# Converting double-precision weights piece by piece: three ScalarE and three VectorE instructions, or two, two and one GpSimd add

## The chip, the core and the metric

The kernel runs on one core of a Trainium2 chip. Five engines work side by side and meet only at semaphores: TensorE (PE in the profile; its weight loads are the row PEld), VectorE (DVE), ScalarE (ACT), GpSimd (POOL) and SyncE (SP), which here only issues DMAs. Each engine takes its instructions strictly in the order in which they stand in its own queue, so an instruction that waits holds everything behind it. The metric is the device time of one execution in microseconds: before the change the median of three runs is 786.03 us (785.67 to 788.26).

## The reference

Two blocks follow each other. The first is a linear-attention recurrence with a 40x40 state for each of 4 batches and 8 heads, over 768 steps. The second is a feed-forward block on the 3072 rows that come out of it, with the hardswish activation.

```python
for t in range(S):                                   # attention, state (B, H, D, D)
    y[:, :, t] = np.einsum('bhd,bhde->bhe', rt, state)
    Sa = np.einsum('bhde,bhe->bhd', state, at)
    state_decay = state * wt[:, :, None, :] - np.einsum('bhd,bhe->bhde', Sa, bt)
    state = state_decay + np.einsum('bhd,bhe->bhde', vt, kt)
...
h = x @ w_in                                         # x (3072, 320), w_in (320, 2048)
g = h * np.clip(h + 3.0, 0.0, 6.0) / 6.0
return (g @ w_out).astype(np.float32)                # w_out (2048, 320)
```

The inputs of the attention are float32. The two weight matrices are float64, since they are scaled by a float64 factor and not cast. The engines work in float32, so the kernel has to turn 2 x 655,360 doubles into float32 on the chip, and this conversion is what the change is about. A double is two 32-bit words: the low word holds 32 bits of the mantissa, the high word the sign, 11 bits of exponent and the top 20 bits of the mantissa.

## The kernel before, in words

**Attention.** The sequence is cut into chunks of 64 steps. A unit is one chunk of two batches; there are 24 units, in groups of `NU` = 4. For each unit `prepare` makes the products that do not need the state (running products of the decay `w` by two scans, lines 571 and 582; scaled `a`, `b`, `k`; score matrices, masked by the predicated copy of line 546), and `step` then carries the state along. For each group of four units a triangular system is inverted on VectorE (`invert`): 30 rounds of a product into `prod` (line 769) and a sum into `x` (line 775), each waiting for the one before, then two 32x32 block transposes (lines 778 and 783) into `tb` and `tt`. `third_block` finishes the inverse into `tinv` with small matmuls.

**Feed-forward.** `expand` multiplies a unit's transposed rows `xt` with `win` and `win2` (line 1124), lines 1139 and 1140 apply the activation into `gt`, and `contract` multiplies with `wout` (line 1165). These matmuls are dealt out between the attention's as soon as a unit and the weights are there.

**Weights.** `weight_pieces` cuts both matrices into `PIECES` = 20 pieces of 128 partitions x 512 doubles; 0 to 4 and 10 to 14 belong to `w_in`, the others to `w_out`. A piece is loaded raw into whatever buffer is free for a while (`raw_homes`: the tiles of `raw`, `tinv`, `F`, `x`, `fb`, `tt`, and parts of `win` and `wout` that are not yet filled), and its float32 values go to their place in `win`, `win2` or `wout`, called `to`. In the raw buffer low and high words alternate, so each is read with a step of 8 bytes. A raw buffer may be loaded again only when the piece in it is finished; the list `free` in `raw_homes` says which piece each later load has to wait for (piece 8 for piece 2, 9 for 3, 10 for 4, 11 for 5, 15 for 8, 16 for 9, 19 for 13). The loads are issued by SP.

Per piece the kernel before runs six instructions of 128 x 512. On ScalarE, `power` makes the power of two of each element in `to`: line 386 scales the top 16 bits down to the exponent field, lines 387 and 388 use Prelu with a huge and a tiny slope to saturate and shift it. On VectorE, line 371 replaces sign-and-exponent bits of the high word by a constant (`tensor_scalar`, two bit operations), line 374 adds the low word times 2^-32 (`scalar_tensor_tensor`), which leaves the mantissa as a float32, and line 362 multiplies it with the power in `to`.

**Order.** Everything is written out by hand; no scheduler moves it. `load_weights` is a generator that yields after `power`, after the last instruction of the piece before, and after each of the two other VectorE instructions. So on VectorE the last instruction of piece n comes right before the first two of piece n+1. The generator is advanced from lists of places: `STEPS` and `POWERS` beside the first inversion, `PLAN` after it, and `by_twos`. The first two pieces and the beginning of the third stand among the 30 rounds of the first inversion. The counters `converted` and `powered` decide at build time when a matmul or a load may stand in a queue.

**Other things on the way.** `seconds` gives a second pair of input tiles `W` and `A` (tile `WA`, in the buffer with the tag `x`, which piece 12 uses before) and has GpSimd fill their padding (line 191). GpSimd also copies scan results (lines 599, 600, 602), keeps the carried decay (lines 869 and 870, which line 871 on VectorE waits for before it scales the state), copies `tb` into `tinv` (lines 818 and 819), clears `U` (line 899), multiplies `KBt` (line 690) and `yg` (line 1054 in the first group, 1029 later).

Of the kernel before, what the change touches and what calls it, by code (L numbers as in the profile page):

```python
# [8 lines left out]
F32 = mybir.dt.float32  # L9
I32 = mybir.dt.int32  # L10
U32 = mybir.dt.uint32
I16 = mybir.dt.int16
ALU = mybir.AluOpType
AF = mybir.ActivationFunctionType
# [3 lines left out]
P = 128  # L18
# [1 line left out]
HB = BL // 2  # L20
L = 32
SLOT = 64
EXP = 916


def _ap(ap, extra, dims):
# [5 lines left out]
def kernel(  # L32
# [42 lines left out]
    nc = tc.nc  # L75
# [12 lines left out]
    const = ctx.enter_context(tc.tile_pool(name="const", bufs=1))  # L88
# [52 lines left out]
    def ps_pair(*dims):  # L141
# [21 lines left out]
        out=ident[:], in_=ones, pattern=[[1, P]],  # L163
# [15 lines left out]
    nc.vector.memset(three[:], 3.0)  # L179
    warm = const.tile([P, 1], F32, name="warm")  # L180
    nc.scalar.activation(out=warm[:], in_=three[:], func=AF.Relu)
    low = const.tile([P, 3], F32, name="low")
    for i, x in enumerate((EXP - 1792.0, -1792.0 * 2 ** 23, -15.0 / 32.0)):
        nc.vector.memset(low[:, i:i + 1], x)


    AHEAD = NU + 1
# [11 lines left out]
    def seconds():  # L199
        t = inv.tile([P, 2, H, SLOT], F32, name="WA1", tag="x", bufs=1)  # L200
        for i, name in enumerate("WA"):
            others[name] = padded(t[:, i], name)
# [58 lines left out]
    for i, (x, y) in enumerate([(0, DFF // 2), (0, NJ // 2)]):  # L261
        for n, z in enumerate((x, y)):
# [4 lines left out]
            name = ("WA", "BK")[i][n]  # L267
# [46 lines left out]
    def load_weights():  # L314

        todo, homes = weight_pieces(), raw_homes()  # L320
        done, issued = [], [0]
        upcoming = []

        def load():
            if issued[0] == min(PIECES, limit[0]):
                return False
            if not upcoming:
                upcoming.append(next(homes))
            raw, before = upcoming[0]
            if before is not None and before not in done:  # L330
                return False
            upcoming.clear()
            issued[0] += 1
            out, loads = next(todo)
            for to, src in loads(raw):
                nc.sync.dma_start(out=to, in_=src)
            loaded.append((out, raw))
            return True

        while load():  # L340
            pass
        refill.append(load)
        phase[0] = 0
        yield
        before = None
        for n in range(PIECES + 1):
            now = None
            if n < PIECES:
                while load():
                    pass  # L350
                out, raw = now = loaded[n]
                hi = raw[:, :, :, 1]
                if powered[0] == n:
                    power()
                    phase[0] = 1
                    yield
            if before:
                to, raw_m = before
                m = raw_m[:, :, :, 1].bitcast(F32)
                if len(to.shape) == 4:  # L360
                    m = m.rearrange("p n (j c) -> p n j c", c=to.shape[3])
                nc.vector.tensor_tensor(out=to, in0=m, in1=to, op=ALU.mult)
                converted[0] += 1
                done.append(n - 1)
                while load():
                    pass
                phase[0] = 2
                yield
            before = now
            if now:  # L370
                nc.vector.tensor_scalar(hi, hi, 0xFFFFF, 0x100000, ALU.bitwise_and, ALU.bitwise_or)
                phase[0] = 3
                yield
                nc.vector.scalar_tensor_tensor(hi.bitcast(F32), raw[:, :, :, 0], 2.0 ** -32, hi, ALU.mult, ALU.add)
                phase[0] = 4
                yield

    def power():

        to, raw = loaded[powered[0]]  # L380
        powered[0] += 1
        top = raw.rearrange("p n c t -> p n (c t)").bitcast(I16)[:, :, 3::4]
        if len(to.shape) == 4:
            top = top.rearrange("p n (j c) -> p n j c", c=to.shape[3])
        bits = to.bitcast(I32)
        nc.scalar.activation(out=bits, in_=top, func=AF.Identity, bias=low[:, 2:3], scale=1.0 / 16.0)
        nc.scalar.activation(out=to, in_=bits, func=AF.Prelu, bias=low[:, 0:1], scale=-1.0, alpha=2.0 ** -40)
        nc.scalar.activation(out=bits, in_=to, func=AF.Prelu, bias=low[:, 1:2], scale=-2.0 ** 63,
                             alpha=2.0 ** -40)

    def weight_pieces():

# [51 lines left out]
    def fetch(name, i, engine=None):  # L444

        if i is None or i >= NK:
            return
        x, crossed = {"W": (w, 0), "A": (a, 0), "B": (b, 0), "K": (k, 0), "R": (r, 1),
                      "V": (v, 1)}[name]
        if name == "V":  # L450
            t = values[i % AHEAD]
        else:
            t = placed.get((name, i))
            if (name, i) == ("R", 1):
                t = others["K"]
            if (name, i) == ("W", NU + 1):
                t = values[NU]
            t = t if t is not None else (others if i < 2 * NU and i % 2 and name != "R" else inputs)[name]
        g, p = names[i]
        engines = engine or nc.sync  # L460
        for q in range(2):
            engine = engines[q] if isinstance(engines, tuple) else engines
            y = x[2 * p + q, :, g * BL:(g + 1) * BL, :]
            rows = slice(q * BL, (q + 1) * BL)
            if crossed:
                for s in range(2):
                    engine.dma_start(out=t[rows, 4 * s:4 * s + 4, 0:D],
                                     in_=y[s::2].rearrange("h t e -> t h e"))
            else:
                engine.dma_start(out=t[rows, :, 0:D], in_=y.rearrange("h t e -> t h e"))  # L470
        data[i][name + "N"] = t
# [890 lines left out]
    for t, line in enumerate(plan):  # L1362
        if t == 8:
            begun_ffn()
            ring.clear()
            ring.extend([("one", 1), ("whole", 2)])
        for name, *amounts in line:
            run(chains[name[0]], 0, 0, *map(int, amounts))
        limit[0] = {3: 15, 8: 17, 9: PIECES}.get(t, limit[0])
        if t == BEGIN - 2:  # L1370
            seconds()
            third.clear()
            second_group = by_twos(NU, 3, 0, 1.25)
        if t == BEGIN:
            fetch("A", NU + 1)
            fetch("W", NU + 3)
        if t == BEGIN + 2:
            fetch("V", NU)
            fetch("V", NU + 1)
            fetch("R", NU)  # L1380
        if t == BEGIN + 1:

            for name in "BK":
                others[name] = second(name)
                fetch(name, NU + 1)
        if t >= BEGIN - 2:
            pieces(3 if t < BEGIN else 1.5 if t < BEGIN + 3 else 0)
        if t >= BEGIN:
            next(second_group)
# [158 lines left out]
```

## Time and profile before

| what | value |
|---|---|
| median of the runs | 786.03 us (785.67 to 788.26, 3 runs) |
| the profiled execution's own time | 785.4 us |
| its span (first to last instruction) | 783.7 us |
| busy in the span: PE, DVE, ACT, POOL | 725.0, 486.6, 320.2, 171.9 us |
| line 362, DVE, 20 instructions | 14.34 us, first at 47.5, last at 131.1 us |
| line 371, DVE, 20 instructions | 408 to 1511 ns, medians 417 to 426 |
| line 374, DVE, 20 instructions | 668 to 978 ns, medians 680 to 698 |
| lines 386, 387, 388, ACT, 20 each | medians about 762, 722, 722 ns |
| lines 1029 and 1054, POOL, 128 x 512 product of two tiles | 1272 ns (20), 1278 and 1606 ns (2) |

Times in views are microseconds from the start of the span; an arrow names who released a wait. A group line gives the line of the program, the engine, the operation, the tiles (written <- read), the shape, the count, the busy time, the mean of one, and the idle time of the engine just before with what ended it. In the row of forty slices each slice is 19.6 us long.

### The profile page before, as it was taken

To read this page: it belongs to the slowest core of one execution; us is meant where nothing else is said; L and a number is where in the kernel's file an instruction comes from. 1 tells how busy PE (TensorE), PEld (TensorE's weight loads), DVE (VectorE), ACT (ScalarE), POOL (GpSimd) and SP (SyncE) were. 2 spreads that over 40 slices of the span, in tenths; PEclk is the share of its full clock that TensorE was granted. 3 is DMA by queue.
4 is the path that set the end of the run, shared out by engine and by line. 5 is a ranking of instruction groups with operands and counts; after the bars stand their busy time and mean duration, and the time that the engine had idled before them with its cause. 6 is when DMAs were issued, how large, how long until landed. Compare 5 with 4: busy or idle time off the path is not lost.

```text
span 783.7 us, 32780 instructions
## 1 busy us (share of the span) xinstructions
PE 725.0 (93%) x14552; PEld 613.3 (78%) x14552; DVE 486.6 (62%) x951; ACT 320.2 (41%) x664; POOL 171.9 (22%) x321
## 2 busy tenths in 40 slices
PE   5636788999999989999999999999999999999998
PEld 3625677878878778888788888888888888888886
DVE  7899967688546699345888336887436972223110
ACT  2386865324445334443334543334543234412211
POOL 6403111222232304121304212203212111110000
PEclk9855899999999999999999999999999999999999
DMA  9684554311333312223213223213221101110000
GB/s 123 116 202 123 113 168 69 68 27 35 58 59 63 67 33 48 50 49 66 41 38 58 46 51 64 44 30 60 49 55 39 26 5 30 30 29 10 12 20 18
DMA packets 174205, 44.87 MB, mean 57 GB/s; under 512 B 157424, under 2 KB 172784, under 8 KB 174064
## 3 DMA queue, kind: packets, MB, share of 16 engines
q1 hardware_dynamic: 169760, 42.03, 27.5%
q8 instruction: 115, 1.88, 1.0%
q10 hardware_dynamic: 4304, 0.74, 0.6%
q14 instruction: 26, 0.21, 0.1%
HBM read 34.08 MB, written 3.93 MB: 49 GB/s over the span
## 4 chain that ended last, share of the span: by engine, by line
PE 77%; DVE 10%; issue 6%; DMA 2%; ACT 2%; POOL 2%; SPq 1%; POOLq 0%; ACTq 0%; DVEq 0%
PE h L1124 27%; PE o L1165 25%; PE pair L1021 4%; PE pair L524 4%; PE pair L496 2%; PE one L486 2%; DVE prods L571 2%; PE pair L884 2%; PE pair L925 1%; PE pair L717 1%; DVE prod L769 1%; PE pair L964 1%; DVE x L775 1%; PE pair L980 1%; PE one L906 1%
## 5 line engine op out<-in xcount | busy, mean ns | idle before, releaser
L1124 PE MATMUL h<-xt,win 128*128 128x128 f32 (+1 forms) x2304 | 248.7, 281 | 4.5 <-DVE gt L1140 4.5
L1124 PEld LDWEIGHTS h<-xt,win 128*128 128x128 f32 (+1 forms) x2304 | 229.3, 191 | 22.6 <-issue 4.2
L1165 PE MATMUL o<-wout,gt 128*128 128x320 f32 x768 | 230.5, 443 | 0.0
L1165 PEld LDWEIGHTS o<-wout,gt 128*128 128x128 f32 x768 | 138.4, 190 | 50.9 <-issue 0.2
L1140 DVE SCALAR_TENSOR_TENSOR gt<-gt,h 128x512 f32<-128x512 f32 x96 | 62.0, 680 | 73.4 <-ACT gt L1139 73.4
L1139 ACT ACTIVATE gt<-h,three 128x512 f32<-128x512 f32 x96 | 62.9, 687 | 102.8 <-PE h L1124 102.3
L546 DVE COPY_PREDICATED area<-mask,pair 128x512 f32<-128x512 int32 x56 | 40.4, 724 | 62.2 <-PE pair L524 52.8
L769 DVE TENSOR_TENSOR prod<-x 128x30 f32<-128x30 f32 (+9 forms) x180 | 65.5, 364 | 8.9 <-POOL x L754 3.3
L775 DVE TENSOR_TENSOR x<-x,prod 128x30 f32<-128x30 f32 (+9 forms) x180 | 64.3, 357 | 5.5
L1029 POOL TENSOR_TENSOR yg<-ys,gam 128x512 f32<-128x512 f32 x20 | 25.4, 1272 | 126.1 <-DVE ys L1028 83.2
L690 POOL TENSOR_TENSOR KBt<-K,rgt 128x320 f32<-128x320 f32 x22 | 19.1, 870 | 151.4 <-ACT rgt L679 139.9
L571 DVE TENSOR_TENSOR_SCAN prods<-area,start 128x528 f32<-128x528 f32 x24 | 40.8, 1703 | 9.7 <-ACT area L567 9.6
L1028 DVE TENSOR_TENSOR ys<-pair,ys 128x512 f32<-128x512 f32 x20 | 13.8, 690 | 49.8 <-PE pair L1021 40.8
L862 ACT ACTIVATE RT<-pair 128x512 f32<-128x512 f32 x22 | 13.1, 597 | 54.5 <-PE pair L496 54.4
L722 ACT ACTIVATE EV<-pair 64x320 f32<-64x320 f32 x44 | 18.9, 430 | 36.9 <-PE pair L717 36.5
L1021 PE MATMUL pair<-area,KBt 64*64 64x104 f32 x1280 | 33.1, 252 | 0.0
L1183 ACT ACTIVATE ob<-o 128x320 f32<-128x320 f32 x22 | 9.6, 437 | 56.2 <-PE o L1165 37.8
L837 ACT ACTIVATE tinv<-pair 32x256 f32<-32x256 f32 x48 | 18.0, 375 | 34.7 <-PE pair L827 34.2
L582 DVE TENSOR_TENSOR_SCAN area<-area,start 128x528 f32<-128x528 f32 x24 | 31.1, 1297 | 0.8
L1021 PEld LDWEIGHTS pair<-area,KBt 64*64 64x64 f32 x1280 | 29.1, 133 | 1.4
L950 POOL COPY area<-V 128x320 f32<-128x320 f32 x20 | 9.1, 455 | 84.6 <-DVE area L612 52.9
L600 POOL COPY rgam<-prods 128x256 f32<-128x256 f32 x22 | 24.9, 1131 | 0.0
(286 smaller groups left out, 1049.9 us busy)
## 6 DMA issues: line engine op xcount, KB each, us to landing
V<-in_v_dram SPq DMA_DIRECT2D x96, 40.0 KB
out_dram<-ob SPq DMA_DIRECT2D x47, 80.0 KB
R<-in_r_dram SPq DMA_DIRECT2D x92, 40.0 KB
B<-in_b_dram SPq DMA_DIRECT2D x42, 80.0 KB
K<-in_k_dram SPq DMA_DIRECT2D x42, 80.0 KB
W<-in_w_dram SPq DMA_DIRECT2D x37, 80.0 KB
A<-in_a_dram SPq DMA_DIRECT2D x37, 80.0 KB
xt<-yg SPq DMA_DIRECT2D x72, 40.0 KB
```

Source lines behind the costliest of these rows:

```text
L524: nc.tensor.matmul(out=o[i][half(q), n ^ (2 * q * placed), :], lhsT=lhs[half(i, D), n ^ (2 * q * swap), half(q)], rhs=rhs[half(i, D), n, h ...
L546: nc.vector.copy_predicated(out=x[:].rearrange("p (i h) t -> p i h t", i=2), mask=mask8, data=o[2])
L571: nc.vector.tensor_tensor_scan(out=prods[:].rearrange("p r m i -> p (r m i)"), data0=wm[:, 0:SCAN], data1=start[:], initial=0.0, op0=ALU.m ...
L582: nc.vector.tensor_tensor_scan(out=back, data0=back, data1=start[:], initial=0.0, op0=ALU.mult, op1=ALU.add)
L769: nc.vector.tensor_tensor(out=pv, in0=_ap(x[:], (i + 1) * L + i, [[L, n], [0, i]]), in1=_ap(x[:], i * L, [[0, n], [1, i]]), op=ALU.mult,)
L775: nc.vector.tensor_tensor(out=rest, in0=rest, in1=pv, op=ALU.add)
L1021: nc.tensor.matmul(out=both[q][half(s), pr, :], lhsT=o[name][half(q), h * D:h * D + SLOT], rhs=beside[name][half(q), 4 * rs + 2 * (s ^ (q ...
L1029: nc.gpsimd.tensor_tensor(out=yg[:], in0=m["ys"][:].rearrange("p r q t -> p r (q t)"), in1=o["G"][:], op=ALU.mult)
L1124: nc.tensor.matmul(out=hp[c][:, i, :], lhsT=lhsT, rhs=rhs, start=(begun[c] == 0), stop=(begun[c] == 3 * NQ - 1))
L1139: nc.scalar.activation(out=gt[:], in_=hp[c][:], func=AF.Relu, bias=three[:], scale=1.0)
L1140: nc.vector.scalar_tensor_tensor(out=gt[:], in0=gt[:], scalar=6.0, in1=hp[c][:], op0=ALU.min, op1=ALU.mult)
L1165: nc.tensor.matmul(out=op[:], lhsT=gts[c][:, n, :], rhs=wout[:, c * HJ + r * NQ + n, :], start=((split or r == 0) and c == 0 and n == 0), ...
```

## The change

The conversion is written in another way, with five instructions per piece.

- On ScalarE, `power` has two copies instead of three activations: the low word times 2^-29 in place (uint32 read, int32 written, so the 3 lowest mantissa bits of the float32 that is to come), and the high word, read as if it were a float32, times 2^-112 into `to`. The second lowers the exponent field so that it fits.
- On VectorE, the first instruction is a `scalar_tensor_tensor`: high word AND sign bit, OR the scaled low word, into the high word. The second is a `tensor_scalar`: `to` shifted left by 3 bits. The third (line 362) is gone.
- On GpSimd, an integer add of the two, `tensor_tensor`, 128 x 512 int32, into `to`, stands where line 362 stood in the program. It is the instruction that finishes the piece.
- The constants in the tile `low` and their three memsets are gone.
- `seconds()` is called two lines of the plan later, at `BEGIN` instead of `BEGIN - 2`.

```diff
-EXP = 916
...
-    low = const.tile([P, 3], F32, name="low")
-    for i, x in enumerate((EXP - 1792.0, -1792.0 * 2 ** 23, -15.0 / 32.0)):
-        nc.vector.memset(low[:, i:i + 1], x)
...
             if before:
                 to, raw_m = before
-                m = raw_m[:, :, :, 1].bitcast(F32)
+                m = raw_m[:, :, :, 1].bitcast(I32)
                 if len(to.shape) == 4:
                     m = m.rearrange("p n (j c) -> p n j c", c=to.shape[3])
-                nc.vector.tensor_tensor(out=to, in0=m, in1=to, op=ALU.mult)
+                nc.gpsimd.tensor_tensor(out=to.bitcast(I32), in0=m, in1=to.bitcast(I32), op=ALU.add)
                 converted[0] += 1
...
             if now:
-                nc.vector.tensor_scalar(hi, hi, 0xFFFFF, 0x100000, ALU.bitwise_and, ALU.bitwise_or)
+                nc.vector.scalar_tensor_tensor(hi, hi, 0x80000000, raw[:, :, :, 0], ALU.bitwise_and, ALU.bitwise_or)
                 phase[0] = 3
                 yield
-                nc.vector.scalar_tensor_tensor(hi.bitcast(F32), raw[:, :, :, 0], 2.0 ** -32, hi, ALU.mult, ALU.add)
+                bits = out.bitcast(U32)
+                nc.vector.tensor_scalar(bits, bits, 3, None, ALU.logical_shift_left)
                 phase[0] = 4
                 yield
...
         to, raw = loaded[powered[0]]
         powered[0] += 1
-        top = raw.rearrange("p n c t -> p n (c t)").bitcast(I16)[:, :, 3::4]
+        lo, hi = raw[:, :, :, 0], raw[:, :, :, 1].bitcast(F32)
         if len(to.shape) == 4:
-            top = top.rearrange("p n (j c) -> p n j c", c=to.shape[3])
-        bits = to.bitcast(I32)
-        nc.scalar.activation(out=bits, in_=top, func=AF.Identity, bias=low[:, 2:3], scale=1.0 / 16.0)
-        nc.scalar.activation(out=to, in_=bits, func=AF.Prelu, bias=low[:, 0:1], scale=-1.0, alpha=2.0 ** -40)
-        nc.scalar.activation(out=bits, in_=to, func=AF.Prelu, bias=low[:, 1:2], scale=-2.0 ** 63,
-                             alpha=2.0 ** -40)
+            hi = hi.rearrange("p n (j c) -> p n j c", c=to.shape[3])
+        nc.scalar.activation(out=lo.bitcast(I32), in_=lo, func=AF.Copy, scale=2.0 ** -29)
+        nc.scalar.activation(out=to, in_=hi, func=AF.Copy, scale=2.0 ** -112)
...
         if t == BEGIN - 2:
-            seconds()
             third.clear()
             second_group = by_twos(NU, 3, 0, 1.25)
         if t == BEGIN:
+            seconds()
             fetch("A", NU + 1)
             fetch("W", NU + 3)
```

## The prediction

> **What bounds the kernel now.** I read the forty slices first, then busy time by stretch, then the chain of waits and the instructions in order of time inside the stretches in which weights are converted (41 to 131 us).
>
> ```profile
> PE   5636788999999989999999999999999999999998
> DVE  7899967688546699345888336887436972223110
> ACT  2386865324445334443334543334543234412211
> POOL 6403111222232304121304212203212111110000
> ```
>
> From about 134 us on TensorE is full. The busy time by stretch shows it in microseconds (columns PE, PEld, DVE, ACT, POOL, granted clock, DMA):
>
> ```profile
> 41.00:61.10 20.10, 5.04 (x80) 4.46 (x80) 18.91 (x52) 16.25 (x25) 0.00 (x0) 0.58 0.85 190
> 61.10:94.40 33.30, 23.76 (x856) 20.85 (x856) 31.43 (x52) 26.16 (x48) 10.81 (x21) 0.70 0.54 128
> 94.40:107.40 13.00, 10.20 (x216) 9.59 (x216) 8.91 (x17) 8.66 (x14) 0.71 (x3) 0.87 0.37 114
> 107.40:134.10 26.70, 24.57 (x480) 21.74 (x480) 21.34 (x36) 14.97 (x25) 3.46 (x5) 0.94 0.49 109
> 134.10:783.70 649.60, 637.12 (x12328) 536.12 (x12328) 371.98 (x729) 240.29 (x522) 134.98 (x231) 1.00 0.22 42
> ```
>
> In the last 650 us TensorE is busy for 637.1, and its queue has the same order in the changed kernel, so a shift of TensorE at 134 us is a shift of the end, one for one. All that can be won or lost lies before. There VectorE is the bound: 18.9 of 20.1 us beside the first inversion, 31.4 of 33.3 us after it. What TensorE waits for says where:
>
> ```profile
> PE lent L804 <- DVE tb L778: 10.1, 1, 10.1
> PE h L1124 <- DVE gt L1140: 2.7, 1, 2.7
> PE lent L1042 <- DVE state L1005: 1.9, 1, 1.9
> ```
>
> The first is the end of the inversion at 61.1 us; the second comes at 107.4 us, behind ScalarE's `gt` and, before it in that queue, six conversion instructions.
>
> **What a GpSimd product does to VectorE.** GpSimd is free (0.00 us busy in 41 to 61.1), so the add has room there. But look at the one product of the same size that runs among conversions, and at VectorE beside it:
>
> ```profile
> 111.43 1.61 POOL L1054 TENSOR_TENSOR yg<-ys,gam 128x512 f32<-128x512 f32 x1 [9.58 <-DMA raw_fb<-in_moe_w_out_dram]
> ...
> 111.21 0.68 DVE L362 TENSOR_TENSOR win<-raw_tt,win 128x512 f32<-128x512 f32 x1
> 111.81 1.51 DVE L371 TENSOR_SCALAR raw<-raw 128x512 uint32<-128x512 uint32 x1
> 113.36 0.69 DVE L374 SCALAR_TENSOR_TENSOR raw<-raw 128x512 f32<-128x512 uint32 x1
> ```
>
> The GpSimd product begins while line 362 runs and takes 1.61 us instead of its usual 1.27; line 371, usually 0.42 us, takes 1.51 and ends when the product has ended. So the two take turns: VectorE lost 1.09 us. The products of line 690 (0.86 us each) do the same to the inversion at 33.9 to 37.3 us, where instructions of 0.27 to 0.29 us take 0.75 to 0.87. Not all of VectorE is hit: line 703, which reads PSUM, keeps its 0.68 us beside line 690 at 32.0, and line 546 its 0.72 at 161.4.
>
> By the Trainium skill, "SBUF — State Buffer", section "SBUF: two separate sides", GpSimd and a VectorE instruction with two SBUF inputs, or in a mode that uses both ports, exclude each other for the whole instruction, and this is the rule that speaks against the change. The rows above agree; with 1.27 instead of 1.09 us for each, the sum below would be about 0.9 us higher.
>
> **The change, part by part.** Unit costs: line 362 takes 0.69 us, but behind a product of the inversion it costs 0.49 us (47.21 to 48.14, against the 0.44 from one round's instruction to the next), elsewhere 0.59 to 0.73 from start to start. Bit operations with two inputs in place of line 371 I take at line 374's 0.60 from start to start, the shift in place of line 374 at line 371's 0.33; within a piece they cancel. The integer add is not in the trace. Nearest is the product of two tiles, 1.27 us (line 1029), which I take, since it also reads two and writes one; the bounds are 0.73 (the one-input copy of line 950, 0.456 us for 320 columns, scaled to 512) and 2.5 (twice the product, as the add also reads with a step of 8 bytes, integers, in place).
>
> 41 to 61.1 us, every instruction on VectorE's chain: adds 0 and 1 each stop the inversion, 2 x 1.09 = +2.2; two line 362 go, -1.0; the third piece's first bit operation stands here and becomes the dearer one, +0.3. Sum **+1.5**.
>
> 61.1 to 79.1: no change. TensorE, at a clock of 0.50, is busy without a gap from 66.2 to 79.6 us and VectorE waits for it at 72.8 and 79.1 (0.72 us); five line 362 go and adds 2 to 6 come inside. If that cover were gone, the five adds less the five products would cost 5 x (1.09 - 0.65), 2.2 us.
>
> 79.1 to 94.4, VectorE without a gap up to the scaled state (line 871, 93.8), which TensorE's line 884 awaits: line 362 of pieces 7, 8 and 9 goes, -0.64 - 0.61 - 0.73; piece 10's first operation, +0.3. Add 7 is followed by two copies from PSUM (0.79 us), which leaves 0.35 of its 1.09; add 8 by lines 1050 and 888, also from PSUM (1.0 us), 0.2; add 9 by a bit operation, 1.09. GpSimd's queue is in order, so line 599's copies (85.1) now stand behind add 8, land on the scan of line 582 and cost about 0.5; line 869, which line 871 awaits, stands behind add 9, inside that add's price. Sum **+0.4**.
>
> 94.4 to 107.4: ScalarE's two pieces take 4.4 us from 101.1 to 105.5. A copy without a bias tile I take at 0.61 us (0.45 for line 878's 320 columns, plus 192 columns at the 0.81 ns by which lines 862 and 563 differ), so two pieces are 1.9 us shorter; but `gt` also needs the matmuls that end at 104.75, so it begins at 104.8 instead of 106.0. Sum **-1.2**.
>
> 107.4 to 134.1: the chain passes VectorE from `gt` (117.4) to the mask of line 546 (122.5): line 362 of piece 16, -0.6; piece 17's first operation, +0.3; add 16, partly behind line 1005 from PSUM, 0.7. Later adds stand beside a wait of 0.4 us. Sum **+0.4**.
>
> Costed at nothing: the three memsets (0.07 us each; VectorE then idles 1.38 us). `seconds()`: the padding of `WA` moves in GpSimd's queue from 100.2 us to behind add 15, about 116; the loads of `WA` do not touch the padding and wait for no GpSimd instruction, and TensorE reads the tile at 125.9. SP's queue keeps its order, but loads into used raw buffers now wait for an add; piece 8's starts at 66.7 us behind piece 2, whose add ends at about the same time as line 362 did, and ScalarE wants it at 82.4. Waits added to GpSimd: each add waits for VectorE and holds the copies, the clearing of `U` and `yg` behind it; of these only line 869 has someone waiting within a microsecond. Without GpSimd's slack each microsecond there would go to line 871.
>
> Total: 1.5 + 0.4 - 1.2 + 0.4 = **+1.1 us** on the profiled execution's 785.4 (span 783.7, 1.7 around it), 786.5. That execution lies 0.6 below the median of 786.03, so the forecast is 787.1 as a median.
>
> **The rivals.** (1) *The integer add is dearer than the float product.* Six adds lie on the path (0, 1, 7, 8, 9, 16), so each microsecond more costs six. From 1.5 us on, the sum passes 2.4 us and the kernel is measurably slower; at 2.0 us it is 787.1 + 6 x 0.73 = 791.5, at 2.5 us 794.5. For it: the form is in no row. Against it: every two-input GpSimd row has the same rate, 2.5 to 2.7 ns a column. The Trainium skill, "GPSIMD Engine Reference", section "Performance pitfalls for Q7 kernels", puts a dearer rate only beyond a step of 8 bytes, which this step does not exceed; no row here has such a step.
>
> (2) *The adds slip in for little, and the kernel is faster.* Without any turn-taking the stretches give -0.7, -1.7, -1.2 and -0.3, -3.9 us: 782.1. The losses I count are 5.0 us; if they come to less than 1.6, a third, it is measurably faster. For it: instructions that read PSUM are not stopped, and a waiting GpSimd may choose its gap. Against it: beside the inversion there is no such instruction for most of the time.
>
> (3) *SP falls behind.* From 106.5 to 154 us it issues nearly without a pause, and TensorE already waits 0.27 us for `B` at 149.8. If add 13 released the last raw buffer 2 us late (104.3 us before), 1.7 us would reach that wait: 788.8. A pause of 1.1 us at 116.3 stands against it.
>
> Beside these, the granted clock falls to half in steps of 3.4 us after pauses; one step more or less is 1.7 us either way.
>
> **How the numbers follow.** About 0.3%, 2.4 us, is what a measurement of this kernel can tell from none. My own sum, within that: 0.40. Rival 1: 0.28, rival 3 or a lost clock step: 0.10, together slower 0.38. Rival 2, with a won clock step: 0.22, faster. The likeliest is 787.1, its own range 784.5 to 788.4. The range of all, 781.8 to 793, leaves out about 0.06 below and 0.09 above (the add near its upper bound).
>
> **What would show it.** Right: line 362's successor on GpSimd at 1.2 to 1.7 us; rounds of the inversion of over 1 us beside the first two adds and line 778 starting at about 62.6; `gt` 1.2 us sooner after the rows have landed; line 1124 waiting 1.5 instead of 2.7 us. Wrong: line 778 before 61, adds above 1.7 us, or a new wait of TensorE for GpSimd or for a load.

## The result and the profile after

The changed kernel takes 790.59 us (median of 20 runs, 787.11 to 795.58), the kernel before in the same comparison 785.54 (20 runs, 783.90 to 788.26). The ratio is 1.0065, with a 95% interval of 1.0050 to 1.0081: about 5.1 us slower. That is inside the wide range on record (781.8 to 793), outside the narrower range of the forecast's own sum (784.5 to 788.4), and more than the 1.1 us forecast as likeliest. The profiled execution of the changed kernel took 790.17 us (span 788.2).

In the changed kernel GpSimd's add is line 358, VectorE's two bit operations are lines 367 and 371, ScalarE's two copies 382 and 383; from there on each line has a number smaller by 6 than before (871 is now 865). The forty slices, as before, of 19.7 us:

```profile
PE   5725789999999989999999999999999999999997
DVE  7899757688546699345898346887435982223110
ACT  2365543233454334453234543334533234412211
POOL 6416434322233303112304122304212201110000
```

The busy time by stretch (the window and its length, then PE, PEld, DVE, ACT and POOL with their counts of instructions, granted clock, DMA share and GB/s), cut where the same instructions stand that ended the stretches shown for the kernel before:

```profile
41.00:62.30 21.30, 5.34 (x80) 4.76 (x80) 20.03 (x50) 12.85 (x22) 2.63 (x2) 0.58 0.73 167
62.30:97.70 35.40, 23.71 (x856) 20.82 (x856) 29.73 (x45) 17.21 (x38) 20.72 (x30) 0.69 0.50 121
97.70:112.90 15.20, 12.10 (x216) 11.26 (x216) 7.43 (x12) 6.50 (x12) 5.68 (x5) 0.78 0.60 186
112.90:138.90 26.00, 23.38 (x480) 20.47 (x480) 20.15 (x30) 10.07 (x20) 11.56 (x13) 1.00 0.32 58
138.90:788.20 649.30, 635.51 (x12328) 535.10 (x12328) 371.74 (x728) 240.04 (x522) 134.80 (x231) 1.00 0.22 42
```

The stretches were 20.1, 33.3, 13.0, 26.7 and 649.6 us long and are now 21.3, 35.4, 15.2, 26.0 and 649.3. The last one keeps its length and its 12,328 matmuls: TensorE's shift at its start is the shift of the end, as the prediction read it. VectorE, which filled the second stretch before (31.4 of 33.3 us), now leaves 5.7 us of it free. It is no longer short of time there; it waits. What TensorE waits for between 60 and 170 us names the new link:

```profile
PE lent L798 <- DVE tb L772: 13.6, 1, 13.6
PE pair L518 <- ACT RT L856: 3.2, 1, 3.2
PE lent L1036 <- issue: 2.0, 1, 2.0
PE pair L711 <- DVE area L540: 1.7, 1, 1.7
PE pair L821 <- ACT zs L806: 1.6, 2, 1.1
PE h L1118 <- issue: 1.6, 1, 1.6
PE pair L1036 <- DVE area L540: 1.5, 1, 1.5
PE h L1118 <- DVE gt L1134: 1.4, 1, 1.4
PE pair L878 <- ACT UT L964: 1.3, 1, 1.3
```

The wait for ScalarE's `RT` was not there before. The instructions of all engines in order of time around it show where it comes from (an idle time stands in brackets, with who ended it):

```profile
92.44 0.69 DVE L367 SCALAR_TENSOR_TENSOR raw<-raw 128x512 uint32<-128x512 uint32 x1
93.05 0.42 DVE L371 TENSOR_SCALAR wout<-wout 128x512 uint32<-128x512 uint32 x1
93.50 0.65 ACT L382 ACTIVATE wout<-wout 128x512 int32<-128x512 uint32 x1 [4.96 <-DVE wout L371]
94.06 0.64 ACT L383 ACTIVATE win<-wout 128x512 f32<-128x512 f32 x1
94.60 0.58 ACT L905 ACTIVATE S<-one 128x512 f32<-128x512 f32 x1
94.78 1.29 POOL L358 TENSOR_TENSOR wout<-raw,wout 128x512 int32<-128x512 int32 x1 [3.70 <-ACT win L383]
95.08 0.59 ACT L856 ACTIVATE RT<-pair 128x512 f32<-128x512 f32 x1
...
95.72 0.69 PE L518 MATMUL pair<-RT,VT 40*64 40x64 f32 x32 [3.25 <-ACT RT L856]
...
96.10 0.69 DVE L367 SCALAR_TENSOR_TENSOR wout<-wout 128x512 uint32<-128x512 uint32 x1 [2.64 <-POOL wout L358]
...
96.71 0.48 DVE L865 TENSOR_TENSOR state<-state,scale 128x320 f32<-128x320 f32 x1
```

Read it from the top. VectorE's shift (line 371, 93.05) writes piece 9 into its place in `wout`. ScalarE has been idle for 4.96 us waiting for that shift, since its next instruction is the in-place copy (line 382) of piece 10. Behind the copy in ScalarE's queue stand `S` and `RT`; `RT` came at 90.19 us before and comes at 95.08, and TensorE waits 3.25 us for it. Meanwhile GpSimd's add of piece 9 (94.78) waits for ScalarE's line 383 of piece 10, and VectorE's next instruction (96.10) waits for that add, so the scaled state comes at 96.71 instead of 93.80 us. In the kernel before, `RT`, ScalarE's first instruction of piece 10 (line 386) and the scaled state stand without an idle time before them:

```profile
90.19 0.59 ACT L862 ACTIVATE RT<-pair 128x512 f32<-128x512 f32 x1
90.67 0.76 ACT L386 ACTIVATE win<-wout,low 128x512 int32<-128x512 int16 x1
...
93.80 0.48 DVE L871 TENSOR_TENSOR state<-state,scale 128x320 f32<-128x320 f32 x1
```

Pieces 9 and 10 have no element in common. Piece 10 lies raw in rows 4 to 7 of `wout`; the destination of piece 9 is columns 256 to 319 of rows 0 to 3 and of rows 8 to 11. Seen as one stretch from first to last element, it brackets the raw piece. That the program's waits go by this stretch is inferred from who waits for whom; the experiments below test it. Before the change only ScalarE and the last VectorE instruction wrote the destination, and both stood in an order in which no engine had to wait for another. Now VectorE's shift writes it ahead of ScalarE's work on piece 10, and the instruction that finishes it is on a third engine.

After the stall TensorE's granted clock is at one half for longer: 0.50 from 98 to 104 us, where the kernel before has 0.50 from 96 to 98 and 0.95 from 98 to 100. The 24 matmuls of `h` on line 1118 take 5.11 us from 99.64; before, the same 24 took 3.84 from 96.12. `gt` starts at 111.46 instead of 105.98 us, the mask at 126.68 instead of 121.77, and the end is 4.5 us later.

### The profile page after: what moved, and what is told of

It is laid out like the page before. It is cut to its first block, busy times and chain, and to the rows that moved or that the text cites. A ratio compares the mean times of both kernels' runs of the same rounds, so it can differ in the third digit from the quotient of the medians.

```text
span 788.2 us, 32774 instructions
## 1 busy us (share of the span) xinstructions
PE 724.7 (92%) x14552; PEld 613.2 (78%) x14552; DVE 483.3 (61%) x928; ACT 300.5 (38%) x644; POOL 197.3 (25%) x341
## 4 chain that ended last, share of the span: by engine, by line
PE 77%; DVE 12%; issue 5%; POOL 2%; ACT 2%; DMA 1%; SPq 1%; DVEq 0%; ACTq 0%; POOLq 0%
PE h L1118 28%; PE o L1159 23%; PE pair L1015 4%; PE pair L518 4%; PE one L480 2%; PE pair L490 2%; DVE prods L565 2%; DVE prod L763 2%; PE pair L878 2%; DVE x L769 2%; DVE area L576 1%; PE pair L919 1%; PE pair L958 1%; PE pair L711 1%; PE pair L974 1%
## 5 line engine op out<-in xcount | busy, mean ns | idle before, releaser
L763 DVE TENSOR_TENSOR prod<-x 128x30 f32<-128x30 f32 (+9 forms) x180 | 67.4, 374 | 9.0 <-POOL x L748 3.4
L565 DVE TENSOR_TENSOR_SCAN prods<-area,start 128x528 f32<-128x528 f32 x24 | 42.5, 1776 | 9.3 <-ACT area L561 9.1
L882 DVE TENSOR_TENSOR RR<-pair,EV 128x320 f32<-128x320 f32 x22 | 10.7, 486 | 22.5 <-PE pair L518 22.3
```

The source lines that it names most:

```text
L565: nc.vector.tensor_tensor_scan(out=prods[:].rearrange("p r m i -> p (r m i)"), data0=wm[:, 0:SCAN], data1=start[:], initial=0.0, op0=ALU.m ...
L763: nc.vector.tensor_tensor(out=pv, in0=_ap(x[:], (i + 1) * L + i, [[L, n], [0, i]]), in1=_ap(x[:], i * L, [[0, n], [1, i]]), op=ALU.mult,)
```

## The experiments

Theory A puts most of the loss down to this wait, theory B to the turns that GpSimd's adds take with VectorE. C and D, later, are two ways to share out the price of the adds. Every ratio is to the kernel before, run beside it. The single runs of a kernel lie 2 to 6 us apart from lowest to highest (8.5 for the changed kernel), and each ratio has an interval of 0.0012 to 0.0019 to either side. So a difference between two ratios is uncertain by about 0.002, and smaller ones are not told apart.

### Piece 9 in two halves

```diff
-nc.gpsimd.tensor_tensor(out=to.bitcast(I32), in0=m, in1=to.bitcast(I32), op=ALU.add)
+for x, y in [(to[:, i], m[:, i]) for i in range(2)] if n - 1 == 9 else [(to, m)]:
+    nc.gpsimd.tensor_tensor(out=x.bitcast(I32), in0=y, in1=x.bitcast(I32), op=ALU.add)
...
-nc.vector.tensor_scalar(bits, bits, 3, None, ALU.logical_shift_left)
+for x in [bits[:, i] for i in range(2)] if n == 9 else [bits]:
+    nc.vector.tensor_scalar(x, x, 3, None, ALU.logical_shift_left)
```

> The changed kernel, but the shift (line 371) and the GpSimd add (line 358) of piece 9 are each written as two instructions, one for each half of its destination in wout, so that neither brackets the rows of wout in which piece 10 lies raw. Nothing else differs. Theory A (a new wait through the shared tile wout: ScalarE's in-place copy of piece 10 waits for VectorE's shift of piece 9, with RT and TensorE behind it): ScalarE's idle time of 4.96 us before that copy goes, the scaled state (96.71 us in the changed kernel) comes 2 to 3 us sooner, the notch in TensorE's clock at 99 to 108 us shrinks, and the time falls from 790.6 to 786 to 788.5 us. Theory B (the turns that GpSimd's adds take with VectorE make the loss, the wait only stands where there was slack): within 0.7 us of the changed kernel, 789.9 to 791.3.

Measured: 788.47 us, ratio 1.0022 (1.0007 to 1.0037), against 1.0065: some 3.4 us of the 5.1 are gone (uncertain by about 1.7), with two instructions more. In its timeline (lines are 2 higher here) ScalarE's in-place copies of pieces 10 (90.50) and 11 (93.97) and `RT` stand without the long wait, and what holds the state is now something else:

```profile
90.50 0.68 ACT L384 ACTIVATE wout<-wout 128x512 int32<-128x512 uint32 x1
...
93.47 0.60 ACT L858 ACTIVATE RT<-pair 128x512 f32<-128x512 f32 x1 [0.26 <-PE pair L482]
93.97 0.69 ACT L384 ACTIVATE wout<-wout 128x512 int32<-128x512 uint32 x1
...
95.05 1.96 POOL L359 TENSOR_TENSOR wout<-raw,wout 128x256 int32<-128x256 int32 x2 [2.39 <-DMA raw_tt<-in_moe_w_in_dram]
...
96.98 0.20 POOL L865 TENSOR_TENSOR scale<-last,dec 128x8 f32<-128x8 f32 x1
97.21 0.49 DVE L867 TENSOR_TENSOR state<-state,scale 128x320 f32<-128x320 f32 x1 [1.49 <-POOL scale L865]
```

The gain is theory A's, at the upper edge of the 786 to 788.5 us that it expected. Of its signs, ScalarE's idle time is gone, and the stretch at half clock is shorter: 0.50 from 100 to 102 us and 0.99 from 102 to 104. The state, though, comes no sooner in this execution (97.21 us; it took 789.13 us as a whole): VectorE waits 1.49 us for GpSimd's small `scale`, which stands behind add 9. So A had the price right and one of its signs, the earlier state, wrong.

### The last instruction back on VectorE, with and without the halves

```diff
-nc.gpsimd.tensor_tensor(out=to.bitcast(I32), in0=m, in1=to.bitcast(I32), op=ALU.add)
+nc.vector.tensor_tensor(out=to.bitcast(U32), in0=m.bitcast(U32), in1=to.bitcast(U32), op=ALU.bitwise_or)
```

> The changed kernel with line 358 on VectorE, as a bitwise OR of the two parts, instead of an integer add on GpSimd. What it computes differs a little: a low part that rounds up to 8 no longer carries into the rest of the mantissa. The shared tile's wait stays. Theory A: the inversion ends 1 us or more sooner (line 772 at about 61.2 instead of 62.3) and no VectorE instruction among the conversions takes over 1 us because of GpSimd, but ScalarE still waits for the shift of piece 9: 788 to 790 us. Theory B: all of the loss goes with the adds: 785.5 us or less.

> Both edits at once: the bitwise OR on VectorE (the same small difference in what is computed) and the shift and the OR of piece 9 in two halves. Theory A: the two gains add up, 784 to 786.5 us, about level with the kernel before or a little under it, since six instructions of 128 x 512 are then five and ScalarE has two copies for three activations. Theory B: the same time as with the OR alone, within 0.7 us.

Measured: the OR alone 789.08 us, ratio 1.0047 (1.0029 to 1.0065); the OR with the halves 785.57, ratio 0.9996 (0.9982 to 1.0010). With the OR alone, no GpSimd add is left, and ScalarE waits as long as ever:

```profile
92.36 0.65 ACT L382 ACTIVATE wout<-wout 128x512 int32<-128x512 uint32 x1 [6.73 <-DVE wout L371]
```

The four kernels make a square, in thousandths over the kernel before:

| | adds on GpSimd | OR on VectorE |
|---|---|---|
| piece 9 whole (the wait) | 6.5 | 4.7 |
| piece 9 in halves | 2.2 | -0.4 |

The first number is from the comparison that gave the result. At 786 us, the wait costs 4.3 to 5.1 thousandths, 3.4 to 4.0 us, in either column; the add on GpSimd in place of an OR on VectorE costs 1.8 to 2.6, 1.4 to 2.0 us, in either row. Each of the four differences is uncertain by about 2 thousandths. Taken together, the wait costs 4.7 and the add 2.2 thousandths, each uncertain by about 1.6, so the second is only just clear of nothing. Theory B is refuted as the main cause: without any GpSimd add, 3.7 us of the loss remain. It is right that the adds cost something.

### The kernel before with its product on GpSimd

```diff
-nc.vector.tensor_tensor(out=to, in0=m, in1=to, op=ALU.mult)
+nc.gpsimd.tensor_tensor(out=to, in0=m, in1=to, op=ALU.mult)
...
         if t == BEGIN - 2:
-            seconds()
...
         if t == BEGIN:
+            seconds()
```

> The kernel before, with line 362's product of mantissa and power moved from VectorE to GpSimd and seconds() called at BEGIN as in the changed kernel; the arithmetic of the conversion stays. So it has the 20 GpSimd instructions of 128 x 512 and what they do to VectorE, but no in-place copy on ScalarE and no VectorE instruction that writes wout before the last one of a piece. Theory A: only the price of the turns, line 778 at about 62.3 instead of 61.1 us and 0.5 to 2 us more at the end, 786 to 787.5. Theory B: nearly all of the loss, 789 to 791.

Measured: 789.12 us, ratio 1.0049 (1.0032 to 1.0066). Theory A missed: 3.9 us, not 0.5 to 2. The experiment was not clean. The product itself, on another engine, now brackets the raw piece 10:

```profile
95.56 1.29 POOL L362 TENSOR_TENSOR wout<-raw,wout 128x512 f32<-128x512 f32 x1 [1.15 <-ACT win L386]
```

```profile
96.88 0.43 DVE L371 TENSOR_SCALAR wout<-wout 128x512 uint32<-128x512 uint32 x1 [1.46 <-POOL wout L362]
```

The first fence is GpSimd's timeline, the second VectorE's. The last run of the study therefore splits this product for piece 9 in the same way.

> The kernel before with line 362's product on GpSimd and seconds() at BEGIN, as in the run with the GpSimd product, and the product of piece 9 written as two, one for each half of its destination. In that earlier run the product of piece 9, now on another engine than the reader of piece 10's raw words, held VectorE for 1.46 us (line 371 at 96.88 us, which waited for GpSimd's line 362) and itself waited for ScalarE's line 386; with two halves neither wait is needed. If the shared tile's wait was part of that run's 1.0049: no such wait, and a ratio of 1.002 to 1.0035, the price of GpSimd's queue and turns alone. If the GpSimd product by itself costs it all: 1.0042 to 1.0056.

Measured: 789.87 us, ratio 1.0044 (1.0027 to 1.0061). VectorE's wait for line 362 is gone, and the time hardly moves: VectorE waits 1.49 us for `scale` in its place. So removing the bracket gains nothing that shows in this kernel, where `scale` holds VectorE next (a gain of up to about 2 us is not excluded). Moving the product costs 3.5 us here with the split (2.1 to 4.8) and 3.9 without. The changed kernel with the halves, which has its adds on GpSimd as well, is 1.7 us slower than the kernel before, so the two stand 1.7 us apart, which is about the uncertainty of the difference. They differ in ScalarE's work (three activations against two copies), and TensorE's wait for `gt` is 2.68 us with the former and 1.54 with the latter. That this makes 1.1 us of the difference is argued from two profiles, not tested.

### Which adds cost

Two mixtures: the OR on VectorE for pieces 0 to 9, or for pieces 0 and 1 alone, and GpSimd's add for the rest, with piece 9 in halves in both.

```diff
+    if n - 1 < 10:            # in the other: n - 1 < 2
+        nc.vector.tensor_tensor(out=x.bitcast(U32), in0=y.bitcast(U32), in1=x.bitcast(U32), op=ALU.bitwise_or)
+    else:
         nc.gpsimd.tensor_tensor(out=x.bitcast(I32), in0=y, in1=x.bitcast(I32), op=ALU.add)
```

> The changed kernel with piece 9 in two halves, and with the last instruction of pieces 0 to 9 as a bitwise OR on VectorE (which differs a little in what it computes, as before); pieces 10 to 19 keep the integer add on GpSimd. It divides the price of GpSimd's adds at about 97 us. Theory C (the price is the two adds beside the inversion and the adds 2 to 9 up to the scaled state, that is all before 97 us): the time of the kernel with OR and halves, ratio to the kernel before 0.998 to 1.001, 784.5 to 786.5 us. Theory D (each add costs about the same, wherever it stands): half of the 2.5 us between the two kernels with halves, ratio about 1.001 or more, 786.8 us or more.

> The changed kernel with piece 9 in two halves, and with the OR on VectorE for pieces 0 and 1 alone, those beside the first inversion; pieces 2 to 19 keep the add on GpSimd. Theory C: line 774's transpose starts at about 61.2 instead of 62.3 us, and 0.9 to 1.3 us of the time go with it, ratio about 1.0010, 786.9 to 787.5 us. If the inversion is covered by what follows (the loads and the scaled state come late for other reasons), the ratio stays at 1.0022 within 0.0005.

Measured: OR for 0 to 9, 786.39 us, ratio 1.0001 (0.9989 to 1.0013); OR for 0 and 1, 786.82 us, ratio 1.0009 (0.9995 to 1.0023). The adds from 10 on cost nothing that shows. By the central values, taking the two beside the inversion away is worth about 1.0 us (1.0022 to 1.0009), and 2 to 9 another 0.6; neither step is larger than the uncertainty of 0.002. The central values are theory C's, but theory D, with about 1.001 or more for the first mixture, is not excluded. In the profile of the second, the transpose starts at 61.73 us, later than expected, and the wait for `scale` stands:

```profile
61.73 1.95 DVE L777 STREAM_TRANSPOSE tb<-x 128x1024 f32<-128x1024 f32 x1
...
95.05 0.49 DVE L870 TENSOR_TENSOR state<-state,scale 128x320 f32<-128x320 f32 x1 [1.49 <-POOL scale L868]
```

### The carried decay ahead of add 9

`scale` and `last` of unit 3 are written earlier, all else as with the halves. In the first attempt they stood ahead of unit 1's `last`, so that unit 3's state was scaled by another factor than the reference's.

```diff
-            scale = tmp.tile([P, 2, NPR], F32, name="scale", bufs=2)
-            nc.gpsimd.tensor_tensor(out=scale[:], in0=last_dec[p][:], in1=dec[:, 0], op=ALU.mult)
-            nc.gpsimd.tensor_copy(last_dec[p][:], dec[:, 1])
+            scale = o["scale"] if i == 3 else keep_decay(o, i)    # keep_decay holds these three
...
+            if i == 3:                 # first attempt, behind the copy of dec
+                keep_decay(o, i)
...
+                if i == 1:             # second, behind unit 1's last
+                    keep_decay(data[3], 3)
```

> The changed kernel with piece 9 in two halves, all adds on GpSimd, and the two small GpSimd instructions of the carried decay of unit 3 (scale and last, lines 863 and 864 of the changed kernel) written right behind the copy of dec that they read, so that they stand ahead of add 9 in GpSimd's queue and not behind it. Theory C: VectorE no longer waits 1.49 us for scale, the state is scaled at about 95.8 instead of 97.2 us, and the time falls by 1 to 1.5 us, ratio about 1.0005 to 1.001. If VectorE or TensorE is late there for another reason, the wait goes to that reason and the ratio stays near 1.0022.

> The same question as the run before it on the carried decay, with the order put right: in that run unit 3's factor was read before unit 1 had set it (so its output was another), here scale and last of unit 3 are written right behind unit 1's last, far ahead of add 9 in GpSimd's queue. Piece 9 in two halves, all adds on GpSimd as integer adds, so the arithmetic is that of the changed kernel. Theory C: no wait of VectorE for scale, TensorE's matmul on the scaled state no later than 97 us, ratio to the kernel before 1.0000 to 1.0010 (785.5 to 787 us), where the halves alone gave 1.0022. If the other run's gain came from the wrong factor's order and not from the queue: 1.0020 or more.

Measured: 786.11 us, ratio 1.0002 (0.9983 to 1.0020), and with the order put right 788.13 us, ratio 1.0028 (1.0013 to 1.0042). The second counts, and it speaks against this part of theory C: its interval leaves out the 1.0000 to 1.0010 that C expected, and the time is no better than with the halves alone (1.0022), though a gain below the uncertainty is not excluded. Its profile, of an execution of 785.99 us, 2.1 below the median, shows the sign that C named. VectorE no longer waits for `scale`, and TensorE's matmul on the state starts at 95.49 us, against 97.85 in the profile with the halves alone, although the scaling takes 1.03 us beside add 9 instead of 0.48:

```profile
94.31 1.03 DVE L874 TENSOR_TENSOR state<-state,scale 128x320 f32<-128x320 f32 x1
```

```profile
95.49 0.68 PE L887 MATMUL pair<-state,at 40*64 40x40 f32 x32 [2.23 <-ACT win L385]
```

TensorE's wait here ends 0.15 us after the scaling (95.34 us), and about the same time lies between the two in the profiles that put this wait down to the state. So it is most likely the state's, though the profile names ScalarE's line 385. What takes the earlier state back in the median is not settled, and neither is why the first attempt ran faster; the two intervals overlap.

### `seconds()` alone, and two candidates

> The kernel before with one edit: seconds() is called at BEGIN instead of BEGIN - 2, as in the changed kernel. All theories here expect no difference: ratio 0.9985 to 1.0015. A difference of 1 us or more would mean that part of what was put down to the conversion belongs to this move.

Measured: 785.79 us, ratio 0.9998 (0.9985 to 1.0011): the move costs nothing. From the program it can be seen why it came with the change: `WA` lies in the buffer that piece 12 uses raw, and its padding is GpSimd work. With the last reader of piece 12 on GpSimd too, a padding written ahead of it in the same queue would wait for an instruction behind it.

The candidates move the first VectorE instruction of piece 10 behind the scaled state, and in the first also `scale` forward. Both have piece 9 in halves; the first has the OR for pieces 0 to 6 and adds from 7 on, the second the OR for all.

```diff
+                if n == 10:
+                    phase[0] = 3
+                    yield
                 nc.vector.scalar_tensor_tensor(hi, hi, 0x80000000, raw[:, :, :, 0], ALU.bitwise_and, ALU.bitwise_or)
-                phase[0] = 3
-                yield
+                if n != 10:
+                    phase[0] = 3
+                    yield
```

> A candidate: the changed kernel with piece 9 in two halves, scale and last of unit 3 early, the OR on VectorE for pieces 0 to 6 and the integer add on GpSimd for 7 to 19, and the first VectorE instruction of piece 10 behind the scaled state instead of ahead of it. By theories A and C together it has none of the three costs found (the wait through wout, the adds beside the inversion, scale behind add 9) and two OR's and a bit operation less on VectorE's chain to the scaled state (about 2 us, less 0.3 to 0.5 for what adds 7 and 8 take back): the state is scaled at 91 to 93 us instead of 93.8 in the kernel before, ratio 0.997 to 0.999, 783.5 to 785.4 us. If TensorE's own work before the state (its clock is 0.5 there) has become the bound, no gain: 0.9995 to 1.0005.

> A candidate without any GpSimd add: the OR on VectorE for all pieces, piece 9 in two halves, and the first VectorE instruction of piece 10 behind the scaled state. Against the kernel with OR and halves it takes 0.6 us off the chain to the scaled state: ratio 0.998 to 0.9995. If that chain is covered by ScalarE's or TensorE's work, as that kernel's wait of TensorE for line 385 at 95.75 us suggests, it stays at 0.9996 within 0.0005.

Measured: 787.16 us, ratio 1.0010 (0.9993 to 1.0027), and 785.75 us, ratio 0.9994 (0.9980 to 1.0008). Neither can be told from the kernel before. Theory A and C's 2 us did not come: in the profile of the first, the slowest of its 12 runs (789.20 us), the state is scaled at 95.83 us, behind a wait of TensorE of 3.01 us at 80.78 us for which the profile names no engine (last section). The second lies in both of the ranges that were expected of it and decides nothing between them. No version here beats the kernel before by more than its scatter.

## Why the prediction was right and where it was wrong

The direction held, though the 1.1 us forecast lay below the 2.4 us that the prediction could tell from none. The wide range held too; the range of the sum itself, 784.5 to 788.4, did not. A time near 790.6 was inside the wide range only for the sake of other mechanisms, above all a dearer add (rival 1, at 0.28), and that one is refuted below. So as far as the mechanism goes, it is luck that the range held. Of the terms of the sum, by the profiled executions:

- *41 to 61.1 us, +1.5.* Right: the transpose of line 772 starts at 62.31 instead of 61.11, +1.2. A product of the inversion beside the add shows the turn:

```profile
44.29 1.32 POOL L358 TENSOR_TENSOR win<-tinv,win 128x512 int32<-128x512 int32 x1 [6.83 <-DMA raw<-in_moe_w_in_dram]
44.49 1.38 DVE L763 TENSOR_TENSOR prod<-x 128x234 f32<-128x234 f32 x1
```

  A round's product usually takes 0.40 us and here 1.38, until the add is over: 0.98 lost, against the 1.09 taken. The exclusive turn for a whole instruction, which the Trainium skill states ("SBUF — State Buffer", section "SBUF: two separate sides"), is what this row shows, to about 0.1 us; not the whole 1.32 is lost, since the add had begun 0.2 us before the product.
- *The add's price.* The 1.27 us taken from the float product were right: 1.29 to 1.32 where nothing is in its way, and more beside VectorE; one of the 20 (1.81 at 78.03 us) passes the 1.7 named as a sign against. Rival 1 is refuted. The 8-byte step costs nothing extra. The Trainium skill ("GPSIMD Engine Reference", section "Performance pitfalls for Q7 kernels") puts a dearer rate only beyond a step of 8 bytes, and these rows agree.
- *61.1 to 79.1 us, 0.* The size came out, by luck: `yg` starts at 80.22 instead of 79.10, the same 1.1 as at the transpose. But the cover that the prediction counted on, TensorE at half clock up to 79.6 us, was not there: the clock is 0.50 only up to 77.5 us in the kernel before, and 1.00 from 74 on in the changed one. VectorE is through with its work ahead of `yg` at 78.74 us, only 0.4 later than before (78.38), and then waits 1.48 us for TensorE, whose matmuls of line 1036 had stood for 2.05 us in a wait for which the profile names no engine (last section). A detail was wrong too: add 2 does not end when line 362 did (66.66 us) but at 68.75, behind GpSimd's copies of `tb`, so that the loads into used raw buffers reach 240 GB/s from 70 us on instead of from 68. No wait for a load was seen to follow in this stretch.
- *79.1 to 94.4 us, +0.4.* Here it failed. The state is scaled 2.9 us later, 1.8 more than at `yg`. The step that failed reads "Waits added to GpSimd: each add waits for VectorE and holds the copies, the clearing of `U` and `yg` behind it; of these only line 869 has someone waiting within a microsecond." It looked for those who wait for GpSimd's queue, and not for the new order between ScalarE, VectorE and GpSimd on one tile. The first copy of a piece now writes its raw words in place, the shift writes the destination early, and for pieces 9 and 10 the two lie interleaved in `wout`. The tiles in which raw pieces lie, `wout` among them, were on the list in the description of the kernel, and the prediction never asked which destination brackets which home.
- *94.4 to 107.4 us, -1.2.* The mechanism was right and was buried. The wait of line 1118 for `gt` is 1.45 us instead of 2.68, where 1.5 was forecast, and the two pieces on ScalarE take 2.1 us less (2.29 from 105.94 to 108.23, against 4.36), where 1.9 was forecast. But `gt` starts 5.5 us later than before. To the 2.9 us of the state come 1.3 us of TensorE's first 24 matmuls at half clock, and a wait of TensorE of 1.56 us at 110.77 us for which the profile names no engine (last section).
- *107.4 to 134.1 us, +0.4, and after 134 nothing.* From the first `gt` to the mask 0.6 us are won rather than 0.4 lost, and on the prediction's own chain, from the second `gt` on VectorE (117.43, now 122.27), 0.1 is lost; at 138.93 TensorE is 4.8 us late, at the end 4.5.
- *Rivals 2 and 3.* The adds do not slip in for little. TensorE's wait for `B` near 150 us is gone, not longer.

Without the wait the sum was near: +1.1 us forecast, and +1.7 (0.6 to 2.9) measured with piece 9 in halves. Part for part, ScalarE's gain less the dearer bit operation was put at -1.2 + 0.9 us, and the kernel with OR and halves stands at -0.3 (-1.4 to +0.8); what is left, the adds for the products, was put at 1.4 (1.2 beside the inversion, 0.1 in each of two later stretches) and measured at 1.4 to 2.0, by the central values about 1.0 of it beside the inversion. Each of these measured values is uncertain by 1 to 2 us, so they agree with the forecast without proving its parts. What the forecast lacked is one term of 3.4 to 4.0 us, the wait. Of the signs named, those of the right side were all seen but the earlier `gt`, and of the wrong ones an add above 1.7 us; the list of wrong signs had new waits of TensorE for GpSimd or a load, and none of ScalarE for VectorE.

## What to carry to other kernels

When an operation changes from one that only reads a buffer to one that writes it in place, or when a destination is written one step earlier or by another engine, list every buffer that shares the tile and ask whether a strided region brackets it: in this kernel the wait followed the bracket, and halving two instructions removed it for almost nothing. An engine with spare time is no cover for such a wait, because of what stands behind it in its queue: ScalarE was idle for 5 us with `RT` behind the waiting copy, and TensorE waited for `RT`. And a wait that is removed is worth only what the next late one leaves: the wait for `scale` was 1.49 us long, and taking it away was worth nothing that could be measured.

## What the hardware showed that was not expected

TensorE seems to stop for its own instructions. The longer waits of TensorE that the profiles put down to "issue" between 70 and 117 us end 1.25 to 1.8 us after a 16 KB packet of the instruction queue has landed. In the changed kernel such packets take 1.31 us from 76.23 and 1.12 us from 108.23:

```profile
79.14 1.04 PE L1036 MATMUL lent<-area,KBt 64*64 64x64 f32 x54 [2.05 <-issue]
...
110.77 0.71 PE L1118 MATMUL h<-xt,win 64*128 64x128 f32 x7 [1.56 <-issue]
```

The DMA queues between 76.2 and 77.6 us show the packet among those of the weights' loads (columns: packets, MB, share of 16 engines):

```profile
q1 hardware_dynamic: 80, 0.26, 83.2%
q8 instruction: 1, 0.02, 5.8%
```

The first wait ends 1.60 us after its packet, the second 1.42. In the kernel with halves the packet begins at 77.83 and ends at 79.04, and TensorE goes on at 80.67, after a wait of 3.09 us; in the candidate with the wait of 3.01 us the packet ends at 79.52, the wait at 80.78. In the kernel before it ends at 76.67, and TensorE, at a granted clock of 0.50 up to 77.5 us, is still busy with line 1042's matmuls until 79.05: no wait. In 11 of the 14 profiles of this study the wait stands at the same place of the program, behind the tenth of these 64 matmuls (line 1036 of the changed kernel), which speaks for the instructions as its cause. That they were late because their packet stood among the loads is likely but was not tested.

The wait lasts between 0 and 3.1 us, one profile for each kernel. It may be part of the scatter, and part of the price of GpSimd's work: it is 2.05 us or more in all six kernels with GpSimd instructions on pieces 0 and 1, and 1.6 or less in the others, but for the candidate with 3.01. Whether the adds cost part of their time through it stays open.
